# A new order for the first two attention blocks, joined attention steps in the later ones, and later preparation around the third phase, in a kernel of one attention and two feed-forward layers

## The chip, the cores and the metric

The kernel runs on one core of a Trainium2 chip. The metric is the device time of one execution in microseconds. A program on the core has five engines with queues of their own, each in order: TensorE (PE: products, into PSUM; its weight loads are shown as PEld), VectorE (DVE), ScalarE (ACT), GpSimd (POOL) and SyncE (SP, which here issues nearly all DMAs). They wait for each other by semaphores.

## The reference, cut to what matters

q, k and v are 8 batches x 8 heads x 576 rows x 64. Keys and values are averaged over 8 rows each, so every row attends to 72 of them.

```python
k_p = k.reshape(B, H, 72, 8, D).mean(axis=3)
v_p = v.reshape(B, H, 72, 8, D).mean(axis=3)
scores = scale * q @ k_p.T            # minus the row's maximum
attn = exp(scores) / (sum(exp(scores)) + 1e-09)
x = attn @ v_p                        # 4608 rows x 512
h = x @ w_in                          # 512 -> 2048
x = maximum(0.01 * h, h) @ w_out      # 2048 -> 512
h = x @ w_in2
g = where(h >= 1, h, where(h <= -1, 0, (h + 1)**2 / 4))
out = g @ w_out2
```

All is in float32.

## The kernel before, in words

Products that matter for precision are split: an operand is cut into a high half in the matmul format fp32r (ACT writes it) and a low half (DVE or POOL: the operand minus its high half), and three products stand for one. Score products, sums of keys and values, and transposes are in plain float32.

There are four phases. In the first, attention and the first layer's input product run block by block: 9 blocks of 512 rows. A block has 32 slots; in each slot TensorE does six products of the first layer (`first`, lines 650 to 652), then what the table of the slot says. While TensorE does the first layer of one block, the attention steps of the next are done. The second phase (`Blocks`, layer 0, line 1206) is the first layer's output product, the third (`first_phase`, line 944) the second layer's input product, the fourth (`Blocks`, layer 1, also line 1206) its output product; these three use a scheme with seven products in place of eight.

An attention step is a Python generator. Each `yield` ends what it issues in one slot; in every slot each running step is moved on once, in the order in which they began (`pump`). A step that begins in slot s thus issues its second part in s + 1, and so on:

- `scores` (line 501 on): two products per part of a tile of 128 rows and four heads; then on DVE the maximum (504) and its subtraction (506); ACT's exponential (514); DVE's sum and reciprocal (519, 520); POOL's multiplication (527). With `by_bias` 1 the subtraction is left to four smaller exponentials on ACT (516).
- `transpose_main` and `transpose_rest`: TensorE turns the attention weights (549, 534), then ACT and DVE cut them (216, 218; 539 to 542).
- `values_to_x`: the values product (566 to 569), then x's halves (258, 260).
- `kv_sum`: DVE sums a block of keys over 8 (416), ACT copies it (418, 419). `values_sum`, `keys_sum`, `rest_sum`: the same sums as products on TensorE (380, 367, 394).
- `weight(f, engine)`: converts one of the 16 input weights from its raw bits: ACT (693, 694), DVE three operations (696, 697, 701), POOL (710), ACT's high half (216), and the low half (218) on DVE for engine 0 or POOL for engine 1. `bits(f)` loads it; three raw buffers take turns.

PSUM has eight banks. Tags "a" and "h" have two each that take turns, "acc0" to "acc3" one each. A step that takes a bank waits until the tile that had it is released. The first layer's results take turns in "h", and ACT evacuates them (658).

For blocks 0 and 1 the order stands in the table `START` (line 23): slot, step, arguments; slots below 0 come before the first product of the first layer. For later blocks it stands in `TIMES` and `attention_of` (597 on), counted back from the slot in which the block's first layer begins. Within a slot, steps are issued in the order of the table.

Near the end of the second phase, `during` (888 on) loads the third phase's first x (`x_load`), forms differences of its quarters on DVE (`x_sum`, line 825) and cuts them into halves (`x_split`: ACT 839, DVE 844), at given units of the phase's last, short pair of row blocks. The seven products of the third phase take them in the order 1, 7, 2, 4, 6, 5, 3 (positions 0 to 6). At the end of the third phase, `after` issues each slot's evacuation and activation steps; for the last cycle they are issued at once, in a loop of six, before the fourth phase's `run` begins to cut its operands (`hi` on ACT, 1169; `lo` on DVE, 1174).

Of the kernel before, what the change touches and what calls it, by code (L numbers as in the profile page):

```python
# [8 lines left out]
F32 = mybir.dt.float32  # L9
# [8 lines left out]
P = 128  # L18
NB = 512
# [1 line left out]
LEAST, MOST = 2.0**-15, 122880.0 - 2.0**-7  # L21

START = (
    (-22, "q_load_first", 0),
    (-20, "kv_load", 0, "k", 0),
    (-20, "kv_load", 0, "k", 1),
    (-20, "kv_load", 0, "k", 2),
    (-20, "kv_load", 0, "k", 3),
    (-20, "rows_load", 0, "v"),
    (-19, "kv_sum", 0, "k", 0),  # L30
    (-19, "kv_sum", 0, "k", 1),
    (-19, "bits", 0),
    (-18, "q_load_first", 1),
    (-18, "kv_sum", 0, "k", 2),
    (-18, "scores", 0, 0, 0, "a", 0),
    (-18, "scores", 0, 0, 1, "acc1", 0),
    (-18, "scores", 0, 0, 2, "a", 0),
    (-17, "kv_sum", 0, "k", 3),
    (-17, "bits", 1),
    (-17, "values_sum", 0, "acc1"),  # L40
    (-16, "scores", 0, 0, 3, "h", 1),
    (-15, "rows_load", 1, "k"),
    (-15, "weight", 0, 1),
    (-15, "scores", 0, 1, 0, "a", 0),
    (-14, "weight", 1, 1),
    (-14, "scores", 0, 1, 1, "h", 0),
    (-14, "bits", 2),
    (-13, "rows_load", 1, "v"),
    (-13, "rest_sum", 0, "acc0"),
    (-12, "keys_sum", 1, "acc2"),  # L50
    (-11, "scores", 0, 1, 2, "a", 1),
    (-11, "scores", 0, 1, 3, "h", 1),
    (-11, "transpose_main", 0, 1, "a"),
    (-10, "transpose_main", 0, 0, "acc1"),
    (-9, "values_sum", 1, "acc3"),
    (-8, "bits", 3),
    (-8, "weight", 2, 1),
    (-7, "weight", 3, 1),
    (-7, "transpose_rest", 0, "acc0"),
    (-6, "q_load", 1, 0, 0),  # L60
    (-6, "q_clear", 1, 0, 0),
    (-6, "rest_sum", 1, "acc2"),
    (-6, "transpose_main", 0, 2, "h"),
    (-5, "bits", 4),
    (-5, "q_load", 1, 0, 1),
    (-4, "values_to_x", 0, 0, "acc1"),
    (-4, "scores", 1, 0, 0, "a", 0),
    (-4, "transpose_main", 0, 3, "acc3"),
    (-4, "values_to_x", 0, 1, "a"),
    (-3, "weight", 4, 0),  # L70
    (-3, "q_load", 1, 0, 3),
    (-2, "bits", 5),
    (-2, "values_to_x", 0, 2, "acc0"),
    (-2, "values_to_x", 0, 3, "acc1"),
    (-1, "q_load", 1, 0, 2),
    (-1, "weight", 5, 0),
    (0, "q_load", 1, 1, 0),
    (0, "scores", 1, 0, 1, "a", 0),
    (0, "bits", 6),
    (0, "scores", 1, 0, 2, "a", 0),  # L80
    (1, "bits", 7),
    (4, "weight", 6, 0),
    (4, "weight", 7, 0),
    (4, "bits", 8),
    (6, "q_load", 1, 1, 1),
    (6, "weight", 8, 0),
    (6, "scores", 1, 0, 3, "a", 0),
    (7, "bits", 9),
    (8, "weight", 9, 0),
    (10, "bits", 10),  # L90
    (10, "weight", 10, 0),
    (10, "bits", 11),
    (10, "scores", 1, 1, 0, "a", 0),
    (10, "q_load", 1, 1, 3),
    (10, "transpose_main", 1, 1, "a"),
    (11, "weight", 11, 0),
    (12, "q_load", 1, 1, 2),
    (12, "bits", 12),
    (13, "transpose_main", 1, 0, "acc1"),
    (13, "scores", 1, 1, 1, "a", 0),  # L100
    (15, "bits", 13),
    (15, "weight", 12, 0),
    (16, "weight", 13, 0),
    (16, "bits", 14),
    (16, "scores", 1, 1, 2, "a", 0),
    (16, "scores", 1, 1, 3, "a", 0),
    (17, "bits", 15),
    (21, "weight", 14, 0),
    (22, "weight", 15, 0),
    (22, "transpose_rest", 1, "a"),  # L110
    (24, "transpose_main", 1, 2, "acc1"),
    (25, "values_to_x", 1, 0, "acc2"),
    (25, "values_to_x", 1, 1, "acc0"),
    (25, "transpose_main", 1, 3, "acc3"),
    (26, "values_to_x", 1, 2, "acc2"),
    (28, "values_to_x", 1, 3, "acc0"),
)

NH = 384
# [1 line left out]
ORDER2 = (4, 5, 7, 6, 1, 3, 2)  # L121

EXPS = 3
KS = 1
UNITS_AHEAD = 10
EARLY = 12
# [20 lines left out]
def attention_moe_moe2(ctx: ExitStack, tc: tile.TileContext, qT, kT, v, k01, v01, w_in1, w_out1, w_in2, w_out2, out):  # L147
# [5 lines left out]
    nc = tc.nc  # L153
# [134 lines left out]
    class Attention:  # L288
        def __init__(self, apool):
# [12 lines left out]
            self.rests = apool.tile([P, NB // P, 8 * REST], F32, name="rests", bufs=1)  # L302
            self.n_exp = 0

        def zero(self):
# [51 lines left out]
            nc.sync.dma_start(out=t, in_=src[b, 4 * P:S])  # L357
            self.raws[b, what, 4] = t

        def keys_sum(self, b, tag):  # L360
            kp = self.sets[b % 2][0]
            ps = ps_tile(tag, f"kps{b}")[:, 0:KT * SP].rearrange("p (i k) -> p i k", i=KT)
            for t in range(5):
                rows = self.raws.pop((b, "k", t))
                n = rows.shape[0]
                for p in range(KT):
                    nc.tensor.matmul(
                        ps[:, p, 16 * t:16 * t + n // 8], rows[:, p * P:(p + 1) * P], self.sums[0:n, 48:48 + n // 8],
                        start=True, stop=True,
                    )  # L370
                yield True
            nc.scalar.activation(out=kp[0:64, :, 0:SP], in_=ps[0:64], func=AF.Copy, scale=1.0 / (POOL * D**0.5))
            nc.scalar.activation(out=kp[64:P, :, SP:], in_=ps[64:P], func=AF.Copy, scale=1.0 / (POOL * D**0.5))
# [118 lines left out]
                        start=i == 0, stop=i == len(parts) - 1,  # L492
                    )

        def scores(self, blk, hf, ti, tag="a", by_bias=0):

            n = P
            ps = ps_tile(tag, f"sc{blk}_{hf}_{ti}")
            self.products(ps, hf, self.q.pop((blk, hf, ti)))
            self.q_clear(blk, *divmod(4 * hf + ti + 1, 4))  # L500
# [85 lines left out]
    def tiles_of(blk):  # L586
# [9 lines left out]

    KV = [("k", 0), ("k", 1), ("k", 2), ("k", 3), ("v", 0), ("v", 1), ("r", 0), ("v", 2), ("v", 3), ("r", 1)]
    TIMES = {
        "kv": (-44, -42, -40, -38, -33, -31, -29, -27, -25, -23), "load": 4,
        "scores": ((-35, -33, -31, -29), (-24, -22, -20, -18)),  # L600
        "rest": -13, "main": (-22, -20, -8, -7), "values": (-10, -9, -5, -4),
    }

    def attention_of(at, blk, known, put):

# [23 lines left out]
        put(TIMES["rest"], at.transpose_rest, blk, "acc0")  # L629
        for p in range(KT):  # L630
            put(TIMES["values"][p], at.values_to_x, blk, p, f"acc{2 - 2 * (p % 2)}")
        for p in range(KT):
            put(TIMES["main"][p], at.transpose_main, blk, p, f"acc{1 + 2 * (p % 2)}")


    x2 = [dram.tile([P, NT], F32, name=f"x2_{e}") for e in range(KT)]
# [121 lines left out]
    class Second:  # L758
# [127 lines left out]
        def during(self, u):  # L886
# [106 lines left out]
        def first_phase(self):  # L993
# [35 lines left out]
            for cycle in range(-1, self.STEPS):  # L1029
                for slot, (prod, ahead) in enumerate(((6, 0), (1, 1), (7, 1), (5, 0), (2, 1), (4, 1), (3, 0))):  # L1030
# [2 lines left out]
                    self.after(cycle, slot)  # L1033
                    for f, args in self.plan.pop((cycle, slot), []):
                        f(*args)
            for slot in range(6):
                self.after(self.STEPS, slot)

        def after(self, c, slot):
            if slot == 0:  # L1040
# [329 lines left out]
            return [lambda: next(steps, None)] * (4 * nb + 3)  # L1370

    with tc.manual_schedule():
        make_identity(nc, ident)
# [3 lines left out]
        apool_cm = tc.tile_pool(name="attn", bufs=1)  # L1377
        at = Attention(apool_cm.__enter__())
        at.zero()
        known = set()  # L1380

# [113 lines left out]
```

## Time and profile before

| | |
|---|---|
| timed runs | 1588.84, 1592.56, 1592.87 us (median 1592.56) |
| profiled execution | 1588.94 us |
| its span | 1587.1 us |
| TensorE products | 1560.0 us busy, 98% of the span, 7920 records |
| DVE | 1207.2 us busy, 76% |
| ACT | 974.2 us busy, 61% |
| POOL | 375.2 us busy, 24% |

The span is what lies between the first and the last instruction; the execution's own time holds 1.8 us more. Rows of an engine give a start and a duration in microseconds from the span's beginning, the line of the kernel, what is written and read, and in brackets the idle time before it and the engine that ended it. The end of a product is modelled, so a busy TensorE isn't one at its peak. One float32 product of the program appears as two records (two passes).

### The profile page before, as it was taken

The numbers are of one execution on the slowest core, as the hardware profiler recorded it, in microseconds if no ns is written. First come the engines' busy times: TensorE is split into PE (matmuls) and PEld (weight loads), VectorE is DVE, ScalarE is ACT, GpSimd is POOL, SyncE is SP. The second block draws the span as 40 slices with busy tenths as digits, with TensorE's granted clock in tenths as the row PEclk, the third lists the DMA queues.
The fourth block names the chain that finished last, engine by engine and source line by source line (L and its number), as shares of the span: only waits on it lengthen the run. The fifth ranks groups of instructions, "written<-read, shape, count | busy, mean of one in ns | idle before, by whom it ended". The sixth has DMA issues, their size and how long they took to land. (4 is left out here: it accounts for less than half of the span.)

```text
span 1587.1 us, 25421 instructions
## 1 busy us (share of the span) xinstructions
PE 1560.0 (98%) x7920; PEld 1363.9 (86%) x7920; DVE 1207.2 (76%) x2361; ACT 974.2 (61%) x2034; POOL 375.2 (24%) x504
## 2 busy tenths in 40 slices
PE   7999999999999999999999999999999999999998
PEld 5778888888888888888889999999999888888888
DVE  7977787787661588999898466777774988778787
ACT  6656556556553456565655688888887645455544
POOL 6533443443330013443430000000000013232210
PEclk9999999999999999999999999999999999999999
DMA  7667787878667788998958667567567989697942
GB/s 240 187 224 266 262 260 248 272 250 266 220 212 279 289 307 224 261 243 238 275 139 306 236 210 259 185 209 247 186 205 235 356 276 215 175 205 186 199 109 67
DMA packets 248201, 366.10 MB, mean 231 GB/s; under 512 B 43969, under 2 KB 126913, under 8 KB 248065
## 3 DMA queue, kind: packets, MB, share of 16 engines
q1 hardware_dynamic: 233696, 339.04, 64.7%
q0 software_dynamic: 13824, 25.17, 9.7%
q8 instruction: 62, 1.02, 0.3%
q14 instruction: 75, 0.61, 0.1%
q10 hardware_dynamic: 544, 0.26, 0.1%
HBM read 196.61 MB, written 142.61 MB: 214 GB/s over the span
## 5 line engine op out<-in xcount | busy, mean ns | idle before, releaser
L1206 PE MATMUL u<-m,v 128*128 128x512 f32 (+1 forms) x3348 | 690.1, 368 | 2.0 <-DVE m L1174 1.7
L1206 PEld LDWEIGHTS u<-m,v 128*128 128x128 f32 x3348 | 583.5, 188 | 108.6 <-DVE m L1174 3.2
L1169 ACT ACTIVATE m<-m 128x512 fp32r<-128x512 f32 (+1 forms) x558 | 327.3, 589 | 300.1 <-PE u L1206 180.6
L1174 DVE TENSOR_TENSOR m<-m,m 128x512 fp32r<-128x512 f32 (+1 forms) x558 | 379.5, 692 | 127.8 <-ACT m L1169 118.2
L1353 POOL TENSOR_TENSOR o<-o,o 128x512 f32<-128x512 f32 x32 | 54.4, 1730 | 632.5 <-DMA m<-g 464.5
L650 PE MATMUL h<-xh,w0i 128*128 128x512 f32 x448 | 181.7, 406 | 2.7 <-ACT t L658 2.7
L652 PE MATMUL h<-xh,w0i 128*128 128x512 f32 x448 | 175.6, 392 | 0.0
L651 PE MATMUL h<-xl,w0i 128*128 128x512 f32 x448 | 175.0, 391 | 0.0
L658 ACT ACTIVATE t<-h 128x512 f32<-128x512 f32 x144 | 86.0, 597 | 100.9 <-PE h L652 58.0
L1151 DVE TENSOR_TENSOR m<-m,m 128x512 f32<-128x512 f32 (+1 forms) x224 | 140.0, 625 | 0.0
L1149 POOL DMA_DIRECT2D m<-m x96 | 84.0, 1017 | 127.1 <-DVE m L1174 91.0
L650 PEld LDWEIGHTS h<-xh,w0i 128*128 128x128 f32 x448 | 84.4, 188 | 18.8 <-ACT t L658 4.0
L652 PEld LDWEIGHTS h<-xh,w0i 128*128 128x128 f32 x448 | 84.1, 188 | 18.2
L651 PEld LDWEIGHTS h<-xl,w0i 128*128 128x128 f32 x448 | 84.3, 188 | 14.8
L944 PE MATMUL V<-xs,v 128*128 128x384 f32 x432 | 87.5, 335 | 0.2 <-DVE xs L844 0.2
L944 PE MATMUL X<-xs,v 128*128 128x384 f32 x432 | 86.4, 334 | 0.0
L944 PE MATMUL Y<-xs,v 128*128 128x384 f32 x432 | 85.3, 334 | 0.0
L527 POOL TENSOR_TENSOR at<-exps,r 128x256 f32<-128x256 f32 x72 | 46.8, 651 | 132.0 <-DVE r L520 105.0
L944 PEld LDWEIGHTS V<-xs,v 128*128 128x128 f32 x432 | 75.7, 188 | 1.4 <-DVE xs L844 1.4
L944 PEld LDWEIGHTS Y<-xs,v 128*128 128x128 f32 x432 | 75.9, 188 | 0.2
L963 DVE TENSOR_TENSOR q<-V,q 128x384 f32<-128x384 f32 x48 | 26.6, 554 | 65.0 <-ACT q L957 65.0
L944 PEld LDWEIGHTS X<-xs,v 128*128 128x128 f32 x432 | 75.9, 188 | 0.0
(261 smaller groups left out, 2516.9 us busy)
## 6 DMA issues: line engine op xcount, KB each, us to landing
m<-g SPq DMA_DIRECT2D x256, 256.0 KB
g<-t SPq DMA_DIRECT2D x144, 256.0 KB
m<-m POOLq DMA_DIRECT2D x96, 256.0 KB, 6.5
wf<-v0o SPq DMA_DIRECT2D x56, 256.0 KB
wi<-v1i SPq DMA_DIRECT2D x56, 256.0 KB
v<-wf SPq DMA_DIRECT2D x28, 512.0 KB
v<-wi SPq DMA_DIRECT2D x28, 512.0 KB
w2d<-w2o SPq DMA_DIRECT2D x56, 256.0 KB
```

The source lines that it names most:

```text
L527: nc.gpsimd.tensor_tensor(out=t.rearrange("p (h k) -> p h k", h=4), in0=e[:, :, c], in1=r.to_broadcast([P, 4, w]), op=ALU.mult)
L650: nc.tensor.matmul(ph, wh[:, c], xh, start=k == 0, stop=False)
L651: nc.tensor.matmul(ph, wh[:, c], xl, start=False, stop=False)
L652: nc.tensor.matmul(ph, wl[:, c], xh, start=False, stop=k == KT - 1)
L658: nc.scalar.activation(out=t, in_=h_t.pop(f), func=AF.Prelu, alpha=0.01)
L944: nc.tensor.matmul(ps, w[:, c], x[k, i], start=begin and k == n == 0, stop=k == 1 and n == 2, skip_group_check=True,)
L1149: nc.gpsimd.dma_start(out=t, in_=x, accum_op=ALU.add)
L1151: nc.vector.tensor_tensor(out=t, in0=x, in1=t, op=ALU.add)
L1169: nc.scalar.activation(out=self.s[u][0], in_=self.unit_source(u), func=AF.Copy)
L1174: nc.vector.tensor_tensor(out=lo, in0=self.unit_source(u), in1=hi, op=ALU.subtract)
L1206: nc.tensor.matmul(banks[b][:, at:at + n], w[:, c], x, start=fresh and at == 0 and i == 0, stop=end and i == 2, skip_group_check=True,)
L1353: engine.tensor_tensor(out=t[:, k], in0=t[:, k], in1=q[:, k], op=ALU.add)
```

## The change

The first two blocks get a new table. Before anything else, three float32 products of zeros (128x128 by 128x512) are issued into a bank that nothing uses yet. A step `scores` can be followed by products of zeros (`fill`); one step of the table has one, all others none. In the later blocks, score tiles 3 and 4 of the first half begin in the same slot, as do 1 and 2 of the second half; the third and fourth main transposes begin in the same slot, two and three slots earlier; the first main transpose two slots earlier; the transposes of the rest one slot later; one sum of values one slot later. The banks stay those of before. In the last pair of the second phase, most of the x steps come later. The last activation steps of the third phase are issued one group behind each of the first six units of the fourth phase.

The table: of its lines up to slot 0, those that the prediction speaks of (the last two numbers of `scores` are by_bias and the fill); loads move by a few slots besides, and the later lines are told below:

```diff
-    (-22, "q_load_first", 0),
-    (-20, "kv_load", 0, "k", 0),
+    (-22, "kv_load", 0, "k", 0),
+    (-20, "q_load_first", 0),
...
-    (-19, "bits", 0),
+    (-19, "kv_sum", 0, "k", 2),
+    (-18, "bits", 0),
     (-18, "q_load_first", 1),
-    (-18, "kv_sum", 0, "k", 2),
-    (-18, "scores", 0, 0, 0, "a", 0),
-    (-18, "scores", 0, 0, 1, "acc1", 0),
-    (-18, "scores", 0, 0, 2, "a", 0),
+    (-18, "scores", 0, 0, 0, "a", 0, 0),
+    (-18, "scores", 0, 0, 1, "acc1", 1, 0),
+    (-18, "scores", 0, 0, 2, "a", 1, 0),
...
-    (-17, "values_sum", 0, "acc1"),
+    (-16, "values_sum", 0, "a"),
...
-    (-15, "weight", 0, 1),
+    (-15, "weight", 0, 0),
...
-    (-14, "scores", 0, 1, 1, "h", 0),
+    (-14, "scores", 0, 1, 1, "h", 0, 1),
...
-    (-11, "scores", 0, 1, 2, "a", 1),
+    (-11, "scores", 0, 1, 2, "a", 0, 0),
...
-    (-6, "transpose_main", 0, 2, "h"),
+    (-4, "transpose_main", 0, 2, "h"),
...
-    (-4, "values_to_x", 0, 1, "a"),
+    (-3, "values_to_x", 0, 1, "a"),
```

From slot 0 on (before -> after): weights 5 at -1 -> 0, 6 at 4 -> 1, 7 at 4 -> 5, 8 at 6 -> 7; the low halves of weights 13 and 14 go to POOL; the load q(1,1,0) goes from slot 0, ahead of `bits` 6, to slot 1 behind it; scores of block 1: (1,0,1) by bias, (1,0,3) at 6 -> 8, (1,1,1) at 13 -> 11, (1,1,2) at 16 -> 15, (1,1,3) at 16 -> 17; main transposes 1 and 0 at 10 and 13 -> 13 and 19, the fourth at 25 -> 24; values 2 and 3 at 26 and 28 -> 29 and 30.

```diff
+        def warm_up(self):
+            self.zeros = f32_tile([P, NB], F32, "zeros")
+            nc.vector.memset(self.zeros, 0.0)
+            ps = ps_tile("acc3", "warm")
+            for _ in range(WARM_UP):
+                nc.tensor.matmul(ps, self.zeros[:, 0:P], self.zeros, start=True, stop=True)
...
-        "kv": (-44, -42, -40, -38, -33, -31, -29, -27, -25, -23), "load": 4,
-        "scores": ((-35, -33, -31, -29), (-24, -22, -20, -18)),
-        "rest": -13, "main": (-22, -20, -8, -7), "values": (-10, -9, -5, -4),
+        "kv": (-44, -42, -40, -38, -33, -31, -29, -26, -25, -23), "load": 4,
+        "scores": ((-35, -33, -31, -31), (-24, -24, -20, -18)),
+        "rest": -12, "main": (-24, -20, -10, -10), "values": (-10, -9, -5, -4),
...
-                (16, self.x_load, 0), (24, self.x_split, 0, 0, 0), (25, self.x_split, 0, 0, 1),
-                (26, self.x_sum, 1), (28, self.x_sum, 3), (30, self.x_sum, 2),
-                (32, self.x_split, 0, 1, 0), (33, self.x_split, 0, 1, 1),
-                (34, self.x_split, 0, 2, 0), (35, self.x_split, 0, 2, 1), (36, self.x_sum, 4),
-                (46, self.x_split, 0, 3, 0), (47, self.x_split, 0, 3, 1),
-                (52, self.x_split, 0, 4, 0), (53, self.x_split, 0, 4, 1),
+                (16, self.x_load, 0),
+                (19, self.x_split, 0, 0, 0),
+                (21, self.x_split, 0, 0, 1),
+                (29, self.x_sum, 1),
+                (32, self.x_sum, 3),
+                (43, self.x_sum, 2),
+                (44, self.x_split, 0, 1, 0),
+                (51, self.x_split, 0, 1, 1),
+                (53, self.x_split, 0, 2, 0),
+                (55, self.x_split, 0, 2, 1),
+                (55, self.x_sum, 4),
+                (55, self.x_split, 0, 3, 0),
+                (55, self.x_split, 0, 3, 1),
+                (55, self.x_split, 0, 4, 0),
+                (55, self.x_split, 0, 4, 1),
...
-            for slot in range(6):
-                self.after(self.STEPS, slot)
+
+        def rest(self, u):
+            if u < 6:
+                self.after(self.STEPS, u)
...
-        l2.b2.run(None)
+        l2.b2.run(l2.rest)
```

## Rows read from the trace of the kernel before

**Rows 1.** The page's first part: busy time, share of the span, instructions.

```profile
PE 1560.0 (98%) x7920; PEld 1363.9 (86%) x7920; DVE 1207.2 (76%) x2361; ACT 974.2 (61%) x2034; POOL 375.2 (24%) x504
```

**Rows 2.** Windows: length; busy PE, PEld, DVE, ACT, POOL; clock, DMA share, GB/s.

```profile
0.00:40.16 40.16, 30.75 (x136) 20.61 (x137) 30.89 (x70) 25.27 (x60) 25.25 (x46) 1.00 0.79 237
40.16:100.00 59.84, 53.20 (x260) 43.22 (x259) 53.30 (x93) 38.53 (x76) 25.43 (x30) 1.00 0.65 202
...
860.00:884.00 24.00, 22.53 (x169) 21.04 (x168) 20.75 (x53) 13.19 (x33) 0.00 (x0) 1.00 0.48 184
```

**Rows 3.** TensorE's waits over the whole span: total us, times, longest.

```profile
PE h L650 <- ACT t L658: 2.7, 3, 1.3
PE tr L534 <- POOL rests L527: 2.1, 2, 1.4
PE u L1206 <- DVE m L1174: 1.7, 5, 0.6
PE sc L490 <- ACT exps L514: 1.6, 2, 0.9
PE tm L549 <- POOL at L527: 1.2, 1, 1.2
PE av L566 <- DVE xl L260: 0.9, 2, 0.5
```

**Rows 4.** Timeline of TensorE in the first 42 us: start, duration, operation.

```profile
11.75 3.78 PE L380 MATMUL vps<-vn,sums 128*128 128x512 f32 x4 [0.59 <-ACT exps L514]
15.32 1.16 PE L490 MATMUL sc<-kp,q 128*128 128x144 f32 x4
...
17.73 0.66 PE L490 MATMUL sc<-kp,q 128*128 128x144 f32 x4
...
41.53 1.15 PE L490 MATMUL sc<-kp,q 128*128 128x144 f32 x8
```

**Rows 5.** Timeline of DVE from 5 to 17 us.

```profile
5.66 0.75 DVE L416 TENSOR_REDUCE ks<-k 128x72 f32<-128x576 f32 x1 [3.21 <-DMA k<-in_kT_dram]
...
16.53 0.46 DVE L504 TENSOR_REDUCE m<-sc 128x4 f32<-128x288 f32 x1 [2.04 <-PE sc L490]
```

**Rows 6.** Timeline of ACT from 13 to 14 us.

```profile
13.70 0.67 ACT L693 ACTIVATE wc0i<-wb0i 128x512 f32<-128x512 f32 x1 [0.33 <-DMA wb0i<-in_moe_w_in_dram]
```

**Rows 7.** DVE's operations by shape, 0 to 100 us: busy, mean ns, idle before.

```profile
L701 DVE SCALAR_TENSOR_TENSOR wc0i<-wb0i,wc0i 128x512 uint32<-128x512 uint32 x16 | 12.6, 790 | 0.6
...
L218 DVE TENSOR_TENSOR w0i<-wc0i,w0i 128x512 fp32r<-128x512 f32 x12 | 10.4, 876 | 0.2
...
L506 DVE TENSOR_TENSOR sc<-sc,m 128x288 f32<-128x288 f32 x13 | 6.1, 467 | 0.4
...
L218 DVE TENSOR_TENSOR aL<-tm,aH 128x512 fp32r<-128x512 f32 x4 | 2.7, 682 | 0.1
```

**Rows 8.** POOL's operations by shape, 0 to 100 us.

```profile
L218 POOL TENSOR_TENSOR w0i<-wc0i,w0i 128x512 fp32r<-128x512 f32 x4 | 5.1, 1276 | 0.5 <-ACT w0i L216 0.5
```

**Rows 9.** Timeline of DVE where the third phase begins.

```profile
884.38 0.56 DVE L844 TENSOR_TENSOR xs<-xr,xs 128x384 fp32r<-128x384 f32 x1 [3.60 <-ACT xs L839]
```

**Rows 10.** Timeline of TensorE where the fourth phase begins.

```profile
1238.96 0.50 PE L1206 MATMUL u<-m,v 128*128 128x512 f32 x1 [0.27 <-ACT m L1169]
...
1239.69 6.68 PE L1206 MATMUL u<-m,v 128*128 128x512 f32 x28 [0.23 <-DVE m L1174]
```

**Rows 11.** Timeline of TensorE in blocks 4 and 6: score tiles.

```profile
214.64 0.66 PE L490 MATMUL sc<-kp,q 128*128 128x144 f32 x4
217.90 0.66 PE L490 MATMUL sc<-kp,q 128*128 128x144 f32 x4
...
341.57 0.66 PE L490 MATMUL sc<-kp,q 128*128 128x144 f32 x4
```

**Rows 12.** Timeline of ACT: the exponentials of the first and last of these.

```profile
216.39 0.41 ACT L514 ACTIVATE exps<-sc 128x288 f32<-128x288 f32 x1
...
347.48 0.41 ACT L514 ACTIVATE exps<-sc 128x288 f32<-128x288 f32 x1 [2.75 <-DVE sc L506]
```

More of the change, by code (lines that the diff above doesn't have):

```diff
@@ L45 @@
+    (-16, "bits", 1),
+    (-16, "scores", 0, 0, 3, "h", 1, 0),
+    (-15, "weight", 0, 0),
+    (-15, "scores", 0, 1, 0, "a", 0, 0),
+    (-14, "rows_load", 1, "k"),
     (-14, "weight", 1, 1),
-    (-14, "scores", 0, 1, 1, "h", 0),
+    (-14, "scores", 0, 1, 1, "h", 0, 1),
     (-14, "bits", 2),
-    (-13, "rows_load", 1, "v"),
-    (-13, "rest_sum", 0, "acc0"),
-    (-12, "keys_sum", 1, "acc2"),
-    (-11, "scores", 0, 1, 2, "a", 1),
-    (-11, "scores", 0, 1, 3, "h", 1),
-    (-11, "transpose_main", 0, 1, "a"),
@@ L54 @@
-    (-10, "transpose_main", 0, 0, "acc1"),
+    (-12, "rows_load", 1, "v"),
+    (-11, "rest_sum", 0, "acc0"),
+    (-11, "keys_sum", 1, "acc2", 0),
+    (-11, "scores", 0, 1, 2, "a", 0, 0),
+    (-11, "scores", 0, 1, 3, "h", 1, 0),
+    (-11, "transpose_main", 0, 0, "acc1"),
+    (-10, "transpose_main", 0, 1, "a"),
+    (-10, "bits", 3),
     (-9, "values_sum", 1, "acc3"),
-    (-8, "bits", 3),
+    (-9, "q_load", 1, 0, 0),
     (-8, "weight", 2, 1),
+    (-7, "transpose_rest", 0, "acc0"),
     (-7, "weight", 3, 1),
-    (-7, "transpose_rest", 0, "acc0"),
@@ L72 @@
     (-2, "bits", 5),
     (-2, "values_to_x", 0, 2, "acc0"),
[L74 to L78, printed above, removed]
+    (-2, "values_to_x", 0, 3, "acc3"),
+    (-2, "q_load", 1, 0, 2),
+    (0, "weight", 5, 0),
+    (0, "scores", 1, 0, 1, "a", 1, 0),
+    (0, "scores", 1, 0, 2, "a", 0, 0),
     (0, "bits", 6),
-    (0, "scores", 1, 0, 2, "a", 0),
-    (1, "bits", 7),
-    (4, "weight", 6, 0),
@@ L83 @@
-    (4, "weight", 7, 0),
+    (1, "q_load", 1, 1, 0),
+    (1, "weight", 6, 0),
+    (3, "bits", 7),
     (4, "bits", 8),
-    (6, "q_load", 1, 1, 1),
-    (6, "weight", 8, 0),
-    (6, "scores", 1, 0, 3, "a", 0),
+    (5, "weight", 7, 0),
     (7, "bits", 9),
+    (7, "weight", 8, 0),
+    (8, "scores", 1, 0, 3, "a", 0, 0),
+    (8, "q_load", 1, 1, 1),
     (8, "weight", 9, 0),
@@ L92 @@
     (10, "bits", 11),
-    (10, "scores", 1, 1, 0, "a", 0),
+    (10, "scores", 1, 1, 0, "a", 0, 0),
     (10, "q_load", 1, 1, 3),
-    (10, "transpose_main", 1, 1, "a"),
     (11, "weight", 11, 0),
+    (11, "scores", 1, 1, 1, "a", 0, 0),
     (12, "q_load", 1, 1, 2),
     (12, "bits", 12),
-    (13, "transpose_main", 1, 0, "acc1"),
-    (13, "scores", 1, 1, 1, "a", 0),
+    (13, "transpose_main", 1, 1, "a"),
     (15, "bits", 13),
     (15, "weight", 12, 0),
[L103 to L106, printed above, removed]
+    (15, "scores", 1, 1, 2, "a", 0, 0),
+    (16, "weight", 13, 1),
+    (17, "scores", 1, 1, 3, "a", 0, 0),
+    (17, "bits", 14),
     (17, "bits", 15),
-    (21, "weight", 14, 0),
+    (19, "transpose_main", 1, 0, "acc1"),
+    (21, "weight", 14, 1),
     (22, "weight", 15, 0),
@@ L123 @@
 EXPS = 3
+WARM_UP = 3
 KS = 1
@@ L303, in __init__, with fill @@
             self.n_exp = 0
+        def warm_up(self):
[4 more added lines that the diff above has]
+                nc.tensor.matmul(ps, self.zeros[:, 0:P], self.zeros, start=True, stop=True)
+        def fill(self, ps, n):
+            for _ in range(n):
+                nc.tensor.matmul(
+                    ps[:, 4 * SP:512], self.zeros[:, 0:P], self.zeros[:, 0:512 - 4 * SP], start=True, stop=True
+                )
         def zero(self):
@@ L358, in rows_load, with keys_sum @@
             self.raws[b, what, 4] = t
-        def keys_sum(self, b, tag):
+        def keys_sum(self, b, tag, fill=0):
             kp = self.sets[b % 2][0]
-            ps = ps_tile(tag, f"kps{b}")[:, 0:KT * SP].rearrange("p (i k) -> p i k", i=KT)
+            bank = ps_tile(tag, f"kps{b}")
+            ps = bank[:, 0:KT * SP].rearrange("p (i k) -> p i k", i=KT)
             for t in range(5):
@@ L370, in keys_sum @@
                     )
+                self.fill(bank, fill)
                 yield True
@@ L493, in products, with scores @@
                     )
-        def scores(self, blk, hf, ti, tag="a", by_bias=0):
+        def scores(self, blk, hf, ti, tag="a", by_bias=0, fill=0):
             n = P
@@ L598, in attention_moe_moe2 @@
     TIMES = {
-        "kv": (-44, -42, -40, -38, -33, -31, -29, -27, -25, -23), "load": 4,
-        "scores": ((-35, -33, -31, -29), (-24, -22, -20, -18)),
-        "rest": -13, "main": (-22, -20, -8, -7), "values": (-10, -9, -5, -4),
+        "kv": (-44, -42, -40, -38, -33, -31, -29, -26, -25, -23), "load": 4,
+        "scores": ((-35, -33, -31, -31), (-24, -24, -20, -18)),
+        "rest": -12, "main": (-24, -20, -10, -10), "values": (-10, -9, -5, -4),
     }
+    BANKS = {"rest": "acc0", "main": ("acc1", "acc3", "acc1", "acc3"), "values": ("acc2", "acc0", "acc2", "acc0")}
     def attention_of(at, blk, known, put):
@@ L628, in attention_of @@
                 put(slot, sc, hf, t)
-        put(TIMES["rest"], at.transpose_rest, blk, "acc0")
+        put(TIMES["rest"], at.transpose_rest, blk, BANKS["rest"])
         for p in range(KT):
-            put(TIMES["values"][p], at.values_to_x, blk, p, f"acc{2 - 2 * (p % 2)}")
+            put(TIMES["values"][p], at.values_to_x, blk, p, BANKS["values"][p])
         for p in range(KT):
-            put(TIMES["main"][p], at.transpose_main, blk, p, f"acc{1 + 2 * (p % 2)}")
+            put(TIMES["main"][p], at.transpose_main, blk, p, BANKS["main"][p])
     x2 = [dram.tile([P, NT], F32, name=f"x2_{e}") for e in range(KT)]
@@ L1372, in attention_moe_moe2 @@
     with tc.manual_schedule():
+        apool_cm = tc.tile_pool(name="attn", bufs=1)
+        at = Attention(apool_cm.__enter__())
+        at.warm_up()
         make_identity(nc, ident)
```

18 lines of the change are left out of this document (6 added, 12 removed).

## The prediction

> **What bounds the kernel now.** I read the busy shares first. TensorE is busy for 98% of the span [rows 1], so a change of order can only give back its idle time, some 27 us, and the products that ran slow. The table of windows then says where the idle time lies: 9.4 us before 40.16, where the first product of the first layer runs, 6.6 us from there to 100, 1.5 us around the end of the second phase [rows 2]. The list of TensorE's waits names the releasers: ACT (evacuations, exponentials), POOL (attention weights), DVE (low halves) [rows 3]. The table of windows also says who stands behind them: DVE is busy for 53.3 of the 59.8 us from 40.16 to 100 [rows 2]; it is the bound there, and ACT and POOL are late because their inputs are. Outside the first 100 us there is little to win. The tail behind 1245 is not touched.
>
> The profiled execution took 1588.94 us, its span 1587.1. The three timed runs are 1588.84, 1592.56 and 1592.87, so this profile stands at the lower of two levels, 3.62 below the median. I make the sum against 1588.94 and add 3.62 for the forecast.
>
> **1. The start, up to the end of the first six first-layer products (41.53 before, where the score products behind them begin [rows 4]).** The first key block is now asked for before the 512 KB of q instead of behind them. DVE waited until 5.66 for the keys [rows 5]. It will start earlier, but the second key block still has q ahead of it, so the first scores gain about half a microsecond at most. The three zero products are six passes of 512 columns; four such passes took 3.78 us at 11.75 [rows 4], so six cost about 5.7 us. They begin when the zeros are written, near 1 us, and end near 7; TensorE had nothing to do until keys were summed, that is until after 5.66, and its first tile needs two of them. Their cover is that idle time, and if it were gone they would cost up to 5.7. What they buy is the clock. [...]
>
> [...] The values' sum takes a bank of tag "a", and the third score tile of the second half waits for it until DVE has cut the low half. The third transpose moves from slot -6 to -4, and the second x moves behind the fourth weight: DVE does that weight's three conversion steps (the longest 0.790 [rows 7], so up to 2.4 us) before the low half that the first layer needs. On SP's queue the loads keep nearly the same order; q(1,1,0), which must wait for a free q tile, moves behind the load of weight 6 instead of holding it up. Net gain 0.5 us. Bounds: 2.2 lost (nothing won at the start, the second x late) and 2.6 won (2.1 and half a microsecond for the earlier keys, nothing given back).
>
> **2. Blocks 0 and 1, from there to 100.** Row by row of the waits [rows 3]. The transposes that waited 1.2 us for POOL stood in the slot in which POOL's multiplication is issued (scores at slot 6, transposes at 10); now scores at 8, transposes at 13: gone. The 1.6 us for exponentials were score tiles that needed the bank of a tile of the same tag; the two at slot 16 are now at 15 and 17: gone, but scores at slot 11 now need the bank whose exponential is issued in slot 10. Of the 0.9 us for x's low half, 0.5 is the third values product, now three slots later: gone. The 2.7 us of first-layer products waiting for ACT's evacuation come from ACT standing behind exponentials that wait for DVE. DVE gets less to do: three score tiles lose their subtraction (0.467 each) and one gets it back; two low halves of weights (0.876) go to POOL and one comes back [rows 7]; together 1.8 us less, and weights 6 to 8 are spread over more slots. I take half of the 2.7, and 1.0 for new bank waits near slots 11 and 13. Gain: 1.2 + 1.6 + 0.5 + 1.35 - 1.0 = 3.6. Bounds: 0 and the whole 6.6 of idle time [rows 2].
>
> On the low halves the row shows that the same DVE operation costs 0.876 with both inputs in SBUF and 0.682 with one in PSUM [rows 7], and 1.276 on POOL [rows 8]. [...]
>
> **3. Blocks 2 to 8.** Two pairs of score tiles and one pair of transposes now start in the same slot: 3 x 7 = 21 joined starts. A lone tile's four products took 0.66, two tiles' eight 1.15 [rows 4]: at most 0.17 each, mostly the modelled end counted once; I take 0.5 in all (0 to 3.6). The transposes of the rest start one slot later; they waited 2.1 us for POOL, of which 1.4 once [rows 3], in block 6 (the other 0.7 is in block 0). Score tiles two slots apart started 3.26 apart [rows 11], a tile being 0.5 of it, so a slot is 1.38: the 1.4 go. The paired transposes at slot -10 write tiles of which one is still read by the values product at -9, so ACT's second split waits for that product; behind it stand two splits and the next evacuation. ACT has time: it is busy 38.5 of 59.8 us in the densest stretch [rows 2], and evacuations have two banks. Gain 1.9.
>
> **4. The end of the second phase.** Eight additions and splits of the third phase's x leave the stretch in which DVE is full (20.75 of 24 us [rows 2]) and go to its last units. TensorE waited 1.7 us for DVE's m [rows 3], all but 0.23 of it there. They land where DVE stood idle for 3.60 us [rows 9]: seven operations of some 0.5 us fit just in time. Gain 1.4, bounds 1.0 lost (the last x late for the fourth product) and 1.5 won.
>
> **5. The end of the third phase.** Five activation steps go behind the first splits of the fourth phase; the waits of 0.27 and 0.23 [rows 10] go, their stores have hundreds of us. Gain 0.5, bounds 0.5 lost and won.
>
> Sum: 0.5 + 3.6 + 1.9 + 1.4 + 0.5 = 7.9; 1588.94 - 7.9 = 1581.0, or 1584.7 at the level of the median.
>
> **Rivals**, their times like the forecast's at the level of the median. *DVE stays the bound.* Then a new order only moves the waits about, and blocks 0 and 1 gain what DVE sheds less what the zeros and new waits cost, say 1.0, while the start loses 1.5 by the late second x. Total 1.0 - 1.5 + 1.9 + 1.4 + 0.5 = 3.3, 1589.3: no change. For it: DVE's share in rows 2. Against it: most waits were places where the distance between two steps was one slot too short, and those distances grew.
>
> [...]
>
> *Slower: the pairs stall every later block.* The second score tile of the first pair takes the bank of the tile two slots ahead, where before four slots lay between. That tile must be through max, subtraction and exponential. From the start of its products to the start of the new tile's lie 3.7 us (two slots and two tiles of 0.5). Before, that tile started at 214.64 and its exponential ended at 216.80, 2.2 us later [rows 11, 12]; with that nothing waits. But another tile of a later block started at 341.57 and its exponential ended at 347.89, 6.3 us [rows 11, 12]. If the tiles concerned fall to that, TensorE waits 2.6 us in each of seven blocks, 18.2: 18.2 - 6.0 = 12.2 slower, 1604.8. It decides from 3.7 us on. Against it: what stands before that tile in DVE's queue has not changed.
>
> **How the numbers follow.** About 4.8 us, 0.3%, is what a measurement of this kernel can tell from no change. Forecast 0.55, DVE stays the bound 0.24, clock falls back 0.12, pairs stall 0.09. The forecast lies on the faster side nearly whole (0.53), the clock's case a little over half (0.07), DVE's case by a small part (0.04): faster 0.64, same 0.27, slower 0.09. Below, the range takes in part 2's upper bound (3.0 more) at the lower level of the runs (3.6 less) and 1.0 of part 1's: 1577. Above, it takes in DVE's case with part 4 lost instead of won (2.4): 1592. The stalled pairs are left out.
>
> **What would show it.** Right: score products of 0.66 or less from the first on; first-layer products beginning within 1.5 us of 40.16; under 4 us of TensorE's idle time from there to 100; no wait for POOL in block 6; none for m near 870. Wrong: TensorE's waits for exponentials in blocks 2 to 8, or idle time of 6 us and more from 40 to 100 with DVE as full as now.

## The result and the profile after

The changed kernel takes 1576.1 us in the median of five runs (1573.96 to 1578.51), the kernel before 1592.34 us (1588.84 to 1592.87): a ratio of 0.9901, 95% interval 0.9885 to 0.9916. The gain, 16.2 us, is twice the forecast of 7.9, and the time lies below the range (1577 to 1592). The same two kernels measured again, on another chip, gave 1577.39 against 1588.29 us, ratio 0.9915 (0.9900 to 0.9930), a gain of 10.9. The two gains differ because the kernel before has two levels of time, some 4 us apart; the ten runs of the changed kernel show one.

The profiled executions: 1588.94 us before, 1576.11 after, spans 1587.1 and 1574.3. The page's first part after, beside [rows 1]:

```profile
PE 1558.6 (99%) x7928; PEld 1363.8 (87%) x7928; DVE 1202.2 (76%) x2359; ACT 973.4 (62%) x2040; POOL 376.1 (24%) x505
```

Nearly the same work, but DVE is busy 5.0 us less. The windows after, beside [rows 2], shifted to the same events (columns as there):

```profile
0.00:38.10 38.10, 32.44 (x145) 20.17 (x146) 31.07 (x72) 25.97 (x63) 23.61 (x45) 1.00 0.86 264
38.10:100.00 61.90, 60.46 (x300) 49.95 (x299) 53.13 (x100) 43.23 (x89) 29.46 (x36) 1.00 0.71 220
849.00:873.00 24.00, 23.17 (x183) 22.57 (x182) 23.22 (x58) 15.22 (x39) 0.00 (x0) 1.00 0.54 202
```

From the first first-layer product to 100 us, TensorE's idle time is 1.4 us in place of 6.6, with DVE nearly as full as before (53.13 of 61.90, 86%, in place of 89%). TensorE's waits after, beside [rows 3]:

```profile
PE sc L506 <- DMA q<-in_qT_dram: 2.0, 1, 2.0
...
PE sc L506 <- ACT kp L435: 1.0, 1, 1.0
PE sc L506 <- POOL q L484: 0.8, 1, 0.8
PE u L1235 <- DVE m L1203: 0.8, 1, 0.8
...
PE h L669 <- DVE xl L261: 0.6, 1, 0.6
PE tm L566 <- ACT exps L531: 0.5, 1, 0.5
```

All six groups of [rows 3] are gone or under 1 us; the 2.7 us for ACT's evacuations, of which the forecast took half, went whole. New are the wait for the second half of q near 14 us, one for a cleared q tile (375 us), and the late low half of the second x (0.6), which the prediction had named.

Where the time went, in the two profiles (us, after less before): the first first-layer product -2.06; from there to the 360th product after it -6.18; from there to the end of phase 1 -1.28; phase 2 and the first 13 products of phase 3 -1.87; the rest of phase 3 -0.36; the tail behind it -1.07. One pair of profiles could not tell how much of this is the change, so the kernel before was profiled four times more. In its five profiles the stretch to the 360th product takes 111.65 to 111.96 us, but phase 3 alone differs by 1.1 us, so the -0.36 there says nothing.

### The profile page after: what moved, and what is told of

Its sections match the earlier page's. It is cut to its first block, busy times and chain, and to the rows that moved or that the text cites. A ratio compares the mean times of both kernels' runs of the same rounds, so it can differ in the third digit from the quotient of the medians.

```text
span 1574.3 us, 25417 instructions
## 1 busy us (share of the span) xinstructions
PE 1558.6 (99%) x7928; PEld 1363.8 (87%) x7928; DVE 1202.2 (76%) x2359; ACT 973.4 (62%) x2040; POOL 376.1 (24%) x505
```

## The experiments

Unless said otherwise a kernel is the one before or the changed one with the named part alone altered. Medians are of all runs. The "shorter level" of a kernel is the median of its runs whose mean granted clock over the run is 0.997 or more; runs at 0.993 to 0.995 are the "longer level". The stretch is that from the first first-layer product to the 360th after it (all of block 0's and most of block 1's first layer), 111.94 us in the profile before; its column gives each profile less that.

| kernel | median, us | ratio to before (95%) | shorter level less that of before, us | runs at the longer level | stretch less 111.94, us |
|---|---|---|---|---|---|
| table_only | 1579.68 | 0.9938 (0.9921 to 0.9954) | -7.5 | 0 of 6 | -6.3 |
| later_only | 1587.96 | 0.9994 (0.9983 to 1.0006) | +0.3 | 2 of 12 | -0.1 |
| x_later | 1586.50 | 0.9990 (0.9977 to 1.0003) | -1.4 | 4 of 12 | 0 |
| act_later | 1587.56 | 0.9992 (0.9979 to 1.0004) | -0.1 | 4 of 12 | 0 |
| whole | 1577.39 | 0.9915 (0.9900 to 0.9930) | -10.3 | 0 of 5 | -6.2 |
| warm_only | 1586.77 | 0.9991 (0.9980 to 1.0003) | -1.1 | 2 of 11 | 0 |
| no_warm | 1577.13 | 0.9918 (0.9903 to 0.9932) | -10.6 | 0 of 4 | -6.2 |
| again | 1588.30 | 0.9993 (0.9982 to 1.0004) | +0.6 | 1 of 11 | 0 |
| old_loads | 1577.13 | 0.9923 (0.9896 to 0.9950) | -10.1 | 0 of 4 | -5.6 |
| shed_only | 1588.05 | 0.9998 (0.9988 to 1.0008) | +0.8 | 0 of 10 | -0.4 |
| start_new | 1585.66 | 0.9982 (0.9973 to 0.9991) | -2.1 | 0 of 11 | -0.4 |
| block1_new | 1585.62 | 0.9973 (0.9961 to 0.9984) | -6.5 | 6 of 10 | -5.5 |
| old_slots | 1576.26 | 0.9919 (0.9907 to 0.9932) | -11.5 | 0 of 5 | -6.1 |
| key_first | 1587.85 | 0.9997 (0.9984 to 1.0009) | 0 | 2 of 12 | 0 |
| q_early | 1577.28 | 0.9930 (0.9913 to 0.9947) | -10.6 | 1 of 6 | -6.2 |

The kernel before, run beside them in five comparisons: medians 1587.95 to 1588.29 us, 34 of 100 runs at the longer level, some 4 us above the others. The row of again is the kernel before against itself: a difference of 0.6 at the shorter level, and 1 of 11 in place of a third at the longer one, come by chance.

**The parts one by one.**

table_only: the new `START` and the zero products; the rest as before.

> The new table for blocks 0 and 1 with its three zero products; the later blocks' slots, the third phase's x and the last activations as before. Theory that the parts add up: the stretch up to block 3's first score tile is 8.2 us shorter here as it is with the whole change, and the rest as before: 8.2 us faster than the kernel before in its profiled execution (1580.7), and 8 to 11 by the medians. Theory that the gain of blocks 0 and 1 needs the later blocks' slots too (the pairs work already in block 2, ahead of block 3): 4 to 6 us faster. As the prediction had it: 4.1 faster.

later_only:

```diff
-        "scores": ((-35, -33, -31, -29), (-24, -22, -20, -18)),
-        "rest": -13, "main": (-22, -20, -8, -7), "values": (-10, -9, -5, -4),
+        "scores": ((-35, -33, -31, -31), (-24, -24, -20, -18)),
+        "rest": -12, "main": (-24, -20, -10, -10), "values": (-10, -9, -5, -4),
```

> Only the later blocks' slots are changed. Parts add up: block 6's wait of 1.4 us for POOL goes and one of 0.8 for a cleared q tile comes: 1.3 us faster (1587.6 beside 1588.9). The slots share in the gain ahead of block 3: 2 to 4 faster. As the prediction had it: 1.9 faster. Pairs stall: over 2 slower.

x_later: the new list in `during` alone.

> Only the third phase's x additions and splits come later. Parts add up: the end of the second phase is 2.2 us shorter, all else as before: 2.2 faster (1586.7 beside 1588.9). As the prediction had it: 1.4 faster, the wait for DVE's m alone. If the 2.2 were an effect of the table that shows only here (the earlier end of another queue): 0.

act_later: `l2.b2.run(None)` becomes `l2.b2.run(l2.rest)`, and the loop of six goes.

> Only the last activation steps of the third phase go behind the first splits of the fourth. Parts add up: 1.1 us faster at the end. As the prediction had it: 0.5 faster. No effect of its own: 0.

The table is the gain. The later slots give nothing: from the end of the stretch to the end of phase 1 they are 1.3 us shorter than the profile before, but so are table_only (1.4), act_later (1.6) and the kernel before itself (1.6), which leave the slots alone. The stretch shows the table's gain, 6.1 to 6.3 us, in six kernels with the whole table, whatever else they contain. The x list is worth 1.4 us by the runs, little more than the 0.6 of again, and 2.6 in its profile; the activations can't be told from nothing by the runs. At the shorter level the four parts sum to 8.7 of the 10.3 us of whole, which the intervals allow.

**The zero products.** whole is the changed kernel again; no_warm has `WARM_UP = 0`; warm_only gives the kernel before the zero products and nothing else; again is the kernel before. In no_warm the one `fill` of the table stays.

> The whole change once more, on the chip on which the other kernels of this call run. The parts add up (medians so far: table -7.5 to -8.3, the others together -1): 8.7 us faster than the kernel before. The parts need each other: 12 to 13 faster, as in the first comparison of the two profiled executions. In either case I expect every run at a granted clock of 0.998 or 0.999 and one level of times, where the kernel before has two, some 4.5 us apart, the longer with a granted clock of 0.994 or 0.995.

> The kernel before with the three zero products alone (its own table, slots, x and activations). Theory that the zero products keep TensorE at its upper level: all runs at 0.998 or 0.999, the longer of the two levels is gone; the first score products 0.15 us each instead of 0.28, DVE goes on 2.1 us earlier at 16.5, and all of it is carried through: 1 to 2 faster at the shorter level, 3 faster by the median. Theory that the start is given back in block 0, whose waits for DVE and ACT take it up: 0 to 0.5 at the shorter level. Theory that the levels have nothing to do with the start: about a third of the runs at 0.995.

> The whole change without the three zero products. If they are what removes the longer level, it is back in about a third of the runs, 4 us above the shorter; if the new order at the start does it, all runs are at 0.998 or more. At the shorter level: if the clock of the start is worth what the trace gives up to the first first-layer product (2.1 us, less what blocks 0 and 1 absorb), 1 to 2 us longer than the whole change; if new distances alone make the gain, no difference.

> The kernel before once more, for a second profile of it. Levels: a third of the runs near 0.995, 4.5 us longer. If the profiled execution is one of these, the trace shows where TensorE is slow: at the start (products of 144 columns at 0.28 us beyond 17 us), or in a stretch of some 10 us elsewhere. If it is at the shorter level: how far two profiles of the same kernel differ by themselves at the stage marks, which I expect to be 1 us at most (block 6's wait of 1.4 us for POOL among it).

Without them the changed kernel is as fast, so the gain is not theirs, nor do they remove the longer level by themselves. What they buy is seen in the first score products: ten passes took 2.77 us at 8.39 in the kernel before and take 1.49 at 8.27 in the profile after. It often does not last: of the nine profiles with them the clock column falls to 0.50 before 17 us in six. Windows of TensorE's clock in warm_only (the value behind POOL's):

```profile
8.00:10.00 2.00, 0.72 (x5) 0.72 (x6) 1.40 (x3) 0.52 (x2) 0.00 (x0) 1.00 1.05 395
10.00:12.00 2.00, 1.38 (x7) 1.03 (x5) 1.93 (x6) 1.10 (x4) 0.00 (x0) 0.50 1.10 304
...
14.00:16.00 2.00, 2.00 (x4) 0.81 (x3) 0.86 (x4) 1.23 (x2) 2.00 (x5) 0.50 1.08 368
```

In whole, the same kernel as the changed one, it falls later, after the wait for q:

```profile
14.00:16.00 2.00, 0.45 (x4) 0.48 (x5) 1.17 (x3) 1.93 (x6) 0.66 (x2) 1.00 1.09 363
16.00:18.00 2.00, 2.00 (x8) 1.25 (x7) 1.93 (x6) 1.19 (x3) 1.30 (x2) 0.66 1.07 388
18.00:20.00 2.00, 2.00 (x7) 1.29 (x5) 1.93 (x4) 0.47 (x2) 1.24 (x3) 0.50 1.09 250
```

0.50 is the lower level: where it stands in again4, a later profile of the kernel before, four passes of 512 columns take 3.78 us (at 31.37); in again the same four, at 1.00, take 1.98 (at 25.62). The first first-layer product runs at 40.05 us in whole, and at 38.10 in the profile of the result, where the clock did not fall. The same holds of the kernel before: 40.16 in its first profile and 38.14 in again, in which the products are fast from 11.56 us on. So a single pair of profiles can't tell a difference of 2 us at the start.

**Load or distance.** old_loads keeps the new order and gives each subtraction and low half of blocks 0 and 1 back to the engine it had; shed_only is the reverse. For example, in old_loads:

```diff
-    (-18, "scores", 0, 0, 1, "acc1", 1, 0),
-    (-18, "scores", 0, 0, 2, "a", 1, 0),
+    (-18, "scores", 0, 0, 1, "acc1", 0, 0),
+    (-18, "scores", 0, 0, 2, "a", 0, 0),
```

> The whole change, but in blocks 0 and 1 each score tile's subtraction and each weight's low half on the engine it had before: DVE gets its 1.8 us back, the new order and distances stay. The stretch from the first first-layer product to the 360th after it (40.16 to 152.10 in the profile of before) is 6.2 us shorter with the change in each of four profiles. Theory that the distances do it: it stays 5 to 6.2 shorter, and the time within 1.5 us of the whole change. Theory that DVE's load does it: only 2 to 4 shorter, time 2 to 4 longer than the whole change.

> The kernel before with the changed kernel's assignment of subtractions and low halves in blocks 0 and 1 alone: DVE gives up 1.8 us, every slot stays. Distances theory: the stretch from 40.16 to 152.10 is 0 to 1 us shorter. Load theory: 2 to 4 shorter, most of it in the products that waited 2.7 us for ACT's evacuation.

Windows over the stretch, first of the kernel before:

```profile
40.16:152.10 111.94, 105.30 (x521) 87.49 (x520) 95.24 (x182) 70.22 (x149) 46.62 (x68) 1.00 0.69 223
```

of old_loads:

```profile
40.01:146.38 106.37, 104.30 (x521) 87.53 (x520) 91.17 (x181) 69.65 (x149) 47.19 (x68) 1.00 0.70 227
```

and of shed_only:

```profile
40.62:152.12 111.50, 105.09 (x521) 87.56 (x520) 93.56 (x179) 70.63 (x152) 48.72 (x70) 1.00 0.70 225
```

The theory that DVE's load does it falls: 1.7 us less on DVE (third number of busy time: 93.56 against 95.24) is worth 0.4 us, while the order alone is worth 5.6. In shed_only the waits for ACT's evacuation stay nearly whole:

```profile
PE h L650 <- ACT t L658: 2.6, 2, 1.3
```

And the order takes 4.1 us off DVE's busy time (91.17) with the operations of before. TensorE's busy time falls by 1.0 as well: the first product behind a wait takes 0.50 us (before, at 56.55) in place of 0.39, so in this trace a wait costs more than its idle time.

**Which half, and the longer level.** start_new takes the new rows ahead of slot 0 (and weight 5 at slot 0 in place of -1), block1_new the others; old_slots is the changed kernel with the old `TIMES`; again2 to again4 are the kernel before.

> Of the whole change only the new table's rows ahead of slot 0 (the zero products among them); the rows from slot 0 on are the old ones, and so are the later blocks' slots, the third phase's x and the activations. Between the first first-layer product and the 360th after it the waits that remain tell which rows made which: theory that each wait goes with the distance of its own steps: the waits for POOL (1.2), for exponentials (1.6) and for ACT's evacuation (2.7), whose steps stand at slots 5 to 24, stay, and the stretch is 0 to 1.5 us shorter. Theory that a smoother start empties DVE's queue ahead of slot 0 and the rest follows: 3 to 6 us shorter. Levels: if a longer level comes of TensorE's waits between 40 and 100 us, about a third of the runs are near 0.995 again; if of the start, none.

> The other half: the new table's rows from slot 0 on, the old rows ahead of it (with the zero products). Own distances: the stretch is 4.5 to 6.2 us shorter, the waits for POOL, exponentials and evacuations gone. Smoother start: 0 to 2 shorter. Levels: if they come of the waits between 40 and 100 us, no run near 0.995; if of the start, a third.

> The whole change without the later blocks' new slots. As the prediction had it: 1.9 us longer than the whole change. If the slots are worth nothing (blocks 2 to 8 were 1.3 to 1.6 us shorter than in the first profile of before in every profile since, new slots or old, the same program too): within 0.5 us of the whole change in the stretch from block 3 to the end of the first phase, and the same time.

> The kernel before, a third profile, to catch one of its executions at the longer level (granted clock 0.995, about a third of them). Theory that the clock falls back in a stretch of blocks 0 and 1 in which TensorE idles: clock column 0.50 for some 8 us between 20 and 110 us, and the first-layer products there at twice their distance. Theory that it is a stretch elsewhere: the clock column shows it. At the shorter level: nothing to see.

> The kernel before, a fourth profile, with the same question as the third.

> The kernel before, a fifth profile, to catch an execution at the longer level (about a third). If caught: the clock column shows 0.50 in one stretch of some 8 us more than at the other level, and the stage marks show 4.5 us lost there.

Each wait goes with the distance of its own steps: block1_new has 5.5 of the 6.2 us and loses the waits for POOL and for evacuations (2.7 to 0.2), though one of 1.5 us for an exponential comes; start_new keeps them (1.2 and 1.7). Which of block1_new's rows does how much was not tested. old_slots is as fast as the changed kernel, and from the end of the stretch to the end of phase 1 0.25 us shorter than whole in its profile; it has not the wait of 0.8 us for the cleared tile. again2 and again3 were at the shorter level. again4, 1592.23 us, was at the longer one. Its windows at the start:

```profile
18.00:20.00 2.00, 2.00 (x11) 1.07 (x11) 1.90 (x6) 1.96 (x5) 1.85 (x3) 1.00 1.10 245
...
22.00:24.00 2.00, 2.00 (x11) 1.99 (x11) 1.89 (x6) 1.04 (x2) 2.00 (x3) 0.50 1.07 327
...
32.00:34.00 2.00, 2.00 (x3) 0.67 (x2) 0.91 (x3) 1.52 (x3) 0.00 (x0) 0.50 0.32 63
34.00:40.00 6.00, 6.00 (x26) 3.45 (x25) 3.02 (x6) 4.00 (x8) 2.56 (x2) 0.87 0.19 66
```

TensorE had been fast since 15 us (four score passes in 0.65 at 15.12) and full since 12 (2.00 us busy in each window of 2.00); near 22 the clock goes to 0.50 and stays there until about 35, through transposes and sums of keys and values. The first first-layer product comes 3.9 us later than in the first profile, the stretch behind it has its usual length. So the longer level is spent at the start, not in the waits of blocks 0 and 1: block1_new, which has those waits no more, has it in 6 of 10 runs. The kernels with the new rows ahead of slot 0 had it in none of 40 runs (41 in the expectation below counts one too many). But shed_only, with the old order, had it in none of 10 either, which at a third would come by chance once in some 60 times, and old_loads, with the new order and the old engines, adds only 4 of the 40. So it is open whether the order or the engines ahead of slot 0 keep it off.

**The order of the first loads.** key_first swaps two rows of the table before; q_early moves one of the new table.

```diff
-    (-22, "q_load_first", 0),
-    (-20, "kv_load", 0, "k", 0),
+    (-22, "kv_load", 0, "k", 0),
+    (-20, "q_load_first", 0),
```

> The kernel before with one change: the first key block is asked for ahead of the first q, as in the new table. In the fifth profile of the kernel before, at the longer level, the clock column falls to 0.50 at 22 us and rises again at 35, and 3.9 us are lost up to the first first-layer product; the four kernels with the new rows ahead of slot 0 and their variants have had no such run in 41. If it is the order of these two loads (the first products come earlier, with other idle time behind them) that decides: no run near 0.995 here. If it is another of the new rows ahead of slot 0: about a third of the runs. At the shorter level 0 to 0.6 us faster, the half microsecond that the prediction gave to the earlier key.

> The whole change with the second half of the first q asked for ahead of the value rows instead of behind the bits of the first weight: TensorE waits 1.2 to 2.7 us for it near 13 to 15 us in the profiles of the whole change, and the clock falls there in some of them. If that wait sets the start: 1 to 2 us faster than the whole change. If the start is bound by what the loads move in all (some 390 GB/s from 10 to 20 us), the wait goes to the value rows or the first weight: no difference, within 0.5.

Neither decides. key_first has the longer level in 2 of 12 runs, so the order of these two loads alone does not remove it; q_early has it in 1 of 6. The swap is worth nothing at the shorter level, and q_early is no faster: its wait for q is 0.3 us, but TensorE waits 2.1 us for a key copy near 8 us (1.0 in the profile after) and 1.5 us for DVE near 22. (The loads moved 330 GB/s from 10 to 20 us in the profile after, and 314 in whole; the 390 of the expectation are single stretches.) No version measured here is faster than the changed kernel; the zero products, or the later slots, can be left out of it at no cost that shows.

## Why the prediction was wrong, point by point

**The level.** I added 3.62 us, by which the profiled execution of before lay under its median, to the forecast. That was no offset that both kernels share: it is the longer level, at which, by their times, four of the five runs of before in the first comparison lie, and which no run with all the new rows ahead of slot 0 shows. Against 1581.0 the changed kernel is 4.9 us low, against 1584.7 it is 8.6.

**1, the start: 0.5 forecast.** Over all profiles the first first-layer product comes at 40.35 us in the median with the old rows (eight, without again4, key_first and the two with zero products) and at 38.81 with the new (seven, without q_early); the late low half gives back 0.8 of the 1.5 us, by the wait that I had named. The size was right, 0.7. No run shows the 2.1 us that the bounds of this part use: in its place the medians differ by 1.5, and in the profile after TensorE waits 2.0 us for the second half of q, which I had not seen. The fast products last in some executions only: the case "clock falls back", with a chance of 0.12, came true in six of the nine profiles with the zero products; it cost some 2 us there (40.05 in whole against 38.10) and not the gain.

**2, blocks 0 and 1: 3.6 forecast, some 7 measured from 41.53 on (6.2 in the stretch, and the 0.8 given back ahead of it).** This is the step that failed: "The 2.7 us of first-layer products waiting for ACT's evacuation come from ACT standing behind exponentials that wait for DVE", with half of it taken for DVE's lighter load. The lighter load is worth 0.4 us, and two of the three waits stay with it (1.34 and 1.25 in shed_only); the order alone takes all but 0.2 of the 2.7. The longest, 1.28 us at 81.48, does stand behind exponentials that wait for DVE, as I had it:

```profile
79.09 0.41 ACT L514 ACTIVATE exps<-sc 128x288 f32<-128x288 f32 x1 [1.24 <-DVE sc L506]
80.01 0.41 ACT L514 ACTIVATE exps<-sc 128x288 f32<-128x288 f32 x1 [0.51 <-DVE sc L506]
80.32 0.62 ACT L216 ACTIVATE w0i<-wc0i 128x512 fp32r<-128x512 f32 x1
80.84 0.59 ACT L658 ACTIVATE t<-h 128x512 f32<-128x512 f32 x1
```

The second longest has another chain. ACT before:

```profile
55.38 0.63 ACT L216 ACTIVATE w0i<-wc0i 128x512 fp32r<-128x512 f32 x1 [1.89 <-POOL wc0i L710]
55.91 0.58 ACT L658 ACTIVATE t<-h 128x512 f32<-128x512 f32 x1
```

TensorE, which waited for that evacuation:

```profile
56.55 0.50 PE L650 MATMUL h<-xh,w0i 128*128 128x512 f32 x1 [1.03 <-ACT t L658]
```

ACT stood behind the high half of a weight, for whose POOL step it waited 1.89 us. POOL, and DVE at the same time:

```profile
51.40 1.43 POOL L710 TENSOR_TENSOR wc0i<-wc0i,wb0i 128x512 uint32<-128x512 uint32 x1
53.98 1.37 POOL L710 TENSOR_TENSOR wc0i<-wc0i,wb0i 128x512 uint32<-128x512 uint32 x1 [1.15 <-ACT w0i L216]
```

```profile
49.81 0.43 DVE L697 TENSOR_SCALAR wc0i<-wc0i 128x512 uint32<-128x512 uint32 x1
...
51.68 1.44 DVE L697 TENSOR_SCALAR wc0i<-wc0i 128x512 uint32<-128x512 uint32 x1
...
54.22 1.69 DVE L697 TENSOR_SCALAR wc0i<-wc0i 128x512 uint32<-128x512 uint32 x1
```

The same operation takes 0.43 us by itself, and 1.69 where it begins beside a POOL operation that ends at 55.35. The one of 1.44 us at 51.68 lies in the chain: the POOL step at 53.98 needs its result, and the 1.0 us by which it is longer than alone is about the whole wait of 1.03. Weights 6 and 7 began in one slot there and 8 two slots later, so the POOL step of one met the DVE step of the next. The new table spreads the weights. ACT's idle time ahead of the high halves, 40 to 100 us, before:

```profile
L216 ACT ACTIVATE w0i<-wc0i 128x512 fp32r<-128x512 f32 x12 | 7.6, 632 | 11.8 <-POOL wc0i L710 11.7
```

and after:

```profile
L217 ACT ACTIVATE w0i<-wc0i 128x512 fp32r<-128x512 f32 x12 | 7.6, 630 | 6.1 <-POOL wc0i L728 6.0
```

This wait alone can also go another way: in start_new, where weights 6 and 7 still begin together and the same DVE operation takes 1.70 us, TensorE does not wait there, for it comes 0.84 us later out of its first six products and the evacuation 0.43 us earlier.

So "DVE is the bound there" was read from a busy time that holds waiting. That the order takes 4.1 us off it is shown by old_loads. Where the 4.1 us lie can be counted in the trace of the stretch, against the shortest duration of each kind of operation: before, DVE's operations are 14.1 us longer than that, of which 13.2 in ones that overlap a POOL operation; in old_loads 10.2 and 9.4. Of the twelve of line 697 on these weights before, the five with no POOL operation beside them take 0.43 us each and the other seven 0.98 in the mean, while DVE's sums of exponentials (line 519) take 0.44 with POOL beside them and 0.45 without. So nearly all of it goes with POOL; a kernel that moves POOL's steps alone was not run. Why the operations get longer there, no run shows. The low halves, 0.876 and 0.682 us in the prediction, show the same: from 20 to 112 us before, the twelve with both inputs in SBUF have a median of 0.689, the longest, 1.592, beside POOL operations, and the four with one input in PSUM a median of 0.688. I had looked at the two low halves only (with them on POOL, shed_only still has 1.7 us less on DVE); the other conversion steps I left out.

The other terms held: the waits for POOL (1.2) and for two tiles' exponentials went (of their 1.6 us 0.94 was the tile at slot 13, not one of the two at 16), and 0.7 us of new waits for exponentials came in place of the 1.0 forecast. The wait of 0.6 us for DVE behind the transposes went too, and 1.0 us of slow restarts, neither of which I had counted. So the term that I took at 1.35 was worth 2.7, and 1.6 us were put at nothing without a reason.

**3, the later blocks: 1.9 forecast, nothing found.** The wait of 1.4 us for POOL in block 6 was one of that execution: with the same program again has 0.5 there and again2 1.1. A wait of 0.8 us for a cleared q tile came. The pairs stalled nothing else; that rival is refuted.

**4, the end of phase 2: 1.4 forecast,** 1.9 to 3.0 in six profiles, 1.4 by the runs of x_later. The waits for m went as said; one of 0.8 us, near 851, came. **5, the end of phase 3: 0.5 forecast,** 1.0 and more in the profiles, nothing that runs can tell.

**"DVE stays the bound"** (1589.3) is refuted by old_loads: a new order alone does not move the waits about, it removes them.

## What to carry to other kernels

Follow each wait back to the start of its chain before giving it a cause: the engine that is late may be idle, behind an operation whose input a third engine makes. A busy time is not work: look at the shortest, the median and the longest duration of one operation, and where they differ look at what the other engines do beside it. Before a forecast is set against a median, ask whether the spread of its runs is one level or two, and whether the change touches the place where the levels part.

## What was not expected of the hardware

One program gives two levels of time, some 4 us apart in 1590; in the one profile taken at the longer level (again4), 3.9 us of it are lost where TensorE's clock falls back in the first 35 us; the run's mean granted clock (0.995 against 0.999) tells them apart. What tips it at 22 us in again4, with TensorE full, no run here shows, nor which of the new rows, or of the moved operations, keeps it off. The fall in whole comes behind a window in which TensorE was busy for 0.45 of 2.00 us; the profile after has 0.90 and 1.13 of 2.00 from 12 to 16 us and no fall, and in again4 TensorE is busy for the whole of each window from 12 to 22 us ahead of it.

The clock column does not show the first slow stretch. It reads 1.00 in the windows from 10 to 16 us both before, where four passes of 512 columns took 3.78 us [rows 4], and in again, where they took 1.98:

```profile
11.56 1.98 PE L380 MATMUL vps<-vn,sums 128*128 128x512 f32 x4 [0.64 <-ACT exps L514]
```

Only durations tell there.
